# Moving an addition tree's first level into accumulating DMAs, and regrouping the score matmuls, in a two-block transformer kernel

## The chip, the cores and the metric

The kernel runs on one core of a Trainium2 chip, as one launch. The metric is device time in microseconds. TensorE (PE in the profile) multiplies matrices and writes PSUM; VectorE (DVE) and ScalarE (ACT) do elementwise work; GpSimd (POOL) and SyncE (SP) issue DMAs here and little else. Each engine takes its own instructions strictly in the order in which the program lists them, so an instruction that waits holds up everything behind it on that engine.

## The reference

With S = 2048 tokens and D = 512 channels, bf16 inputs:

```python
def _A_ref(x, wqkv, wo):              # 32 heads of 16 channels
    W, dil = 8, 2
    qkv = (x @ wqkv).reshape(B, S, 3, H, Dh) ...
    idx = pos[:, None] - (jnp.arange(W) * dil)[None, :]
    logits = einsum("bhsd,bhswd->bhsw", q, k[idx]) * Dh ** -0.5   # -1e9 where idx < 0
    o = einsum("bhsw,bhswd->bhsd", softmax(logits), v[idx])
    return o.reshape(B, S, D) @ wo
def _B_ref(x, W_gate, W_up, W_down):  # F = 1376
    gate = x @ W_gate; gate = gate * (gate > 0)
    return (gate * (x @ W_up)) @ W_down
h  = x + _A_ref(layernorm(x), wqkv, wo)
h2 = h + _B_ref(layernorm(h), W_gate, W_up, W_down)
```

Every token attends to eight earlier tokens, at distances 0, 2, ..., 14, in each of 32 small heads.

## The kernel before

The sequence is cut into four chunks of 512 tokens (`tk` 0 to 3). Channels lie on the 128 partitions in four groups `t`, so a chunk of q, k or v is 128 x 4 x 512. For each chunk the stages are:

- First layernorm: statistics by `bn_stats` on DVE (line 390), the reciprocal root by Ln and Exp on ACT (lines 400 to 407), the normalisation itself on DVE (line 425) for chunk 0 and on ACT (line 422, with the small bias made by DVE on line 411) for chunks 1 to 3, then transposes on PE (line 456) and a copy out of PSUM. `LNA` says which engine normalises: its first tuple is for this layernorm, its second for the one after attention.
- q, k and v: 48 matmuls of 128 x 512 (line 502), each group of four evicted by ACT (line 510).
- Scores: because the heads are small, q times shifted k is formed on DVE, for two channel groups and four shifts at a time (line 549, 128 x 4096 elements; four of these a chunk, two for each half `hf` of the eight shifts). PE then sums the channels of each head with a 128 x 32 selector (line 555). There are eight such matmuls for each DVE product, placed on four column strips of the array (`tile_position`), and the two products of a half accumulate in one PSUM bank.
- Softmax: Exp on ACT (line 571), the sum over shifts on PE (line 588), the reciprocal by Ln and Exp on ACT (lines 591 and 594). For chunks in `EARLY` (1 to 3) the weights are scaled by the reciprocal on DVE (line 603), for chunk 0 the result is (line 644).
- Attention output: PE spreads the weights over the channels (line 616, four row strips of the array), ACT copies them to SBUF (line 622), DVE multiplies with eight shifted copies of v for each channel group `t` (line 637, 128 x 4096) and sums the eight shifts by a tree of additions of 2048, 1024 and 512 elements (lines 640 and 663). The first addition of the tree puts the upper half of the product's buffer onto its lower half.
- Output projection (line 683) and residual. For chunks in `RPE` (chunk 0 before) the residual is added on PE with an identity matmul (line 686), and ACT copies the result to `x_sm` and sums its rows (line 692). For the others DVE adds the residual and sums the rows in one instruction out of PSUM (line 694).
- Second layernorm (its square pass on ACT, line 360), then gate and up matmuls (line 721, 88 a chunk), their evictions on ACT (lines 725 and 728), the product on DVE (line 741), the down projection (line 758), the last residual on DVE (line 769) and the store (line 773).

The order on each engine is not the order of this list. `Plan.order()` is a list scheduler: every step has an engine, an assumed duration, dependencies, buffers that it takes, and a priority out of the table `RANK` (one number for each step). Its result is written out as the program's order, so the gate, up and down matmuls of an earlier chunk stand between the attention steps of a later one, and on DVE the products `gT` of line 741 stand between attention steps. Buffers are few: nine `quad`, five `big` (the 128 x 4096 products and the spread weights), two `up_sb`, two `gr`, eight PSUM banks shared by all.

All DMAs before are issued by SP and ACT: loads at the start, all within the first 31 us, and 17 stores of the output (two of 64 KB, the rest 128 KB).

Of the kernel before, what the change touches and what calls it, by code (L numbers as in the profile page):

```python
# [8 lines left out]
P = 128  # L9
# [6 lines left out]


RANK = [
    4, 1, 5, 2, 0, 3, 47, 6, 7, 29, 171, 229, 201, 272, 727, 10, 12, 8, 11, 14,
    17, 23, 28, 32, 20, 26, 31, 16, 18, 21, 24, 27, 34, 37, 9, 13, 15, 19, 22, 25,  # L20
    30, 33, 35, 40, 45, 42, 46, 57, 38, 43, 49, 52, 56, 61, 59, 66, 70, 78, 63, 68,
    67, 74, 75, 99, 84, 157, 136, 167, 73, 180, 72, 94, 88, 101, 109, 114, 65, 83, 87, 95,
    102, 122, 165, 209, 212, 121, 131, 129, 149, 127, 134, 144, 139, 153, 151, 156, 179, 210, 222, 226,
    164, 174, 196, 206, 224, 169, 183, 200, 216, 219, 187, 202, 208, 213, 218, 237, 247, 240, 249, 230,
    238, 233, 239, 254, 267, 255, 263, 242, 258, 243, 260, 270, 273, 282, 292, 276, 283, 295, 278, 286,
    280, 287, 291, 310, 320, 319, 327, 313, 323, 316, 324, 331, 308, 333, 302, 329, 305, 332, 299, 318,
    336, 345, 361, 352, 364, 337, 360, 330, 356, 366, 328, 351, 335, 353, 342, 354, 322, 349, 359, 358,
    381, 368, 389, 363, 384, 365, 387, 393, 355, 391, 348, 382, 399, 395, 417, 709, 733, 429, 434, 716,
    736, 371, 403, 706, 732, 406, 413, 714, 735, 44, 51, 36, 50, 39, 48, 41, 53, 55, 60, 64,
    76, 81, 71, 80, 86, 82, 85, 69, 77, 89, 105, 112, 97, 107, 108, 116, 96, 104, 125, 133,  # L30
    130, 137, 128, 135, 113, 126, 143, 344, 161, 271, 140, 338, 154, 312, 124, 141, 146, 152, 192, 132,
    147, 150, 163, 195, 205, 234, 245, 264, 252, 296, 306, 301, 307, 304, 265, 284, 300, 288, 298, 350,
    362, 370, 374, 309, 321, 339, 347, 340, 367, 372, 376, 314, 326, 334, 377, 386, 397, 390, 402, 383,
    388, 380, 385, 401, 404, 405, 407, 396, 400, 392, 398, 410, 414, 420, 426, 416, 422, 430, 419, 423,
    424, 427, 432, 440, 467, 455, 476, 454, 471, 464, 480, 486, 449, 463, 437, 457, 441, 460, 448, 461,
    466, 468, 481, 439, 465, 472, 484, 451, 469, 489, 446, 473, 458, 487, 443, 477, 462, 488, 491, 475,
    501, 479, 502, 485, 507, 482, 504, 525, 492, 512, 490, 508, 528, 495, 531, 718, 737, 521, 550, 722,
    740, 516, 535, 720, 738, 547, 552, 724, 741, 62, 90, 58, 92, 54, 91, 79, 93, 98, 100, 110,
    155, 159, 145, 158, 162, 142, 148, 119, 138, 160, 198, 220, 181, 217, 176, 214, 184, 223, 166, 228,
    172, 232, 170, 231, 186, 236, 189, 444, 173, 456, 203, 379, 168, 450, 235, 244, 259, 268, 315, 227,  # L40
    256, 257, 279, 317, 325, 343, 346, 357, 409, 369, 408, 418, 411, 394, 412, 428, 436, 435, 425, 447,
    478, 494, 498, 459, 470, 493, 497, 438, 442, 445, 452, 453, 474, 483, 496, 500, 505, 511, 519, 503,
    510, 506, 515, 509, 513, 522, 523, 514, 517, 518, 520, 527, 532, 537, 541, 538, 544, 549, 542, 545,
    534, 539, 551, 585, 606, 554, 583, 572, 603, 569, 600, 612, 564, 579, 568, 581, 555, 575, 560, 576,
    584, 574, 595, 570, 594, 562, 598, 566, 591, 602, 559, 588, 578, 608, 557, 586, 601, 611, 614, 589,
    624, 605, 636, 596, 621, 593, 619, 639, 580, 641, 610, 643, 648, 625, 655, 729, 745, 615, 650, 726,
    742, 637, 654, 728, 743, 633, 657, 730, 746, 111, 118, 106, 117, 115, 123, 103, 120, 175, 177, 178,
    190, 197, 185, 193, 204, 188, 194, 182, 191, 199, 248, 262, 211, 250, 207, 241, 215, 253, 221, 275,
    274, 290, 225, 277, 246, 281, 289, 499, 251, 556, 261, 565, 269, 561, 266, 294, 293, 341, 375, 285,
    303, 297, 311, 373, 378, 415, 421, 431, 524, 433, 530, 533, 536, 526, 529, 540, 548, 546, 543, 553,  # L50
    573, 582, 590, 558, 577, 587, 597, 567, 592, 599, 607, 563, 571, 604, 609, 620, 631, 613, 618, 616,
    623, 617, 628, 634, 635, 622, 626, 627, 629, 630, 632, 638, 640, 651, 652, 645, 649, 656, 642, 646,
    644, 647, 653, 662, 676, 658, 670, 667, 679, 660, 673, 690, 674, 693, 688, 696, 668, 681, 664, 683,
    699, 669, 692, 672, 687, 685, 689, 680, 686, 697, 665, 678, 677, 684, 661, 675, 659, 671, 694, 663,
    701, 666, 703, 682, 710, 691, 705, 712, 695, 704, 698, 708, 711, 707, 717, 734, 749, 700, 719, 739,
    750, 702, 715, 731, 747, 713, 721, 744, 751, 723, 725, 748, 752,
]


# [33 lines left out]
class Plan:  # L93
# [9 lines left out]
    def add(self, key, *a, **k):  # L103
        op = Op(*a, **k)
        op.key = key
        op.seq = len(self.ops)
        if RANK:
            op.prio = RANK[op.seq]
        self.ops.append(op)
        for b in set(op.take) | set(op.use):  # L110
            b.left += 1
        return op
# [57 lines left out]
def kernel(  # L170
# [134 lines left out]


    PESUM = ()
    NWARM = 48
    DMAT = ()

    EARLY = (1, 2, 3)

    RPE, OPE = (0,), ()

    MERGE = ()

    BCN = 4

    LNA = ((0, 1, 1, 1), (0, 0, 0, 0))


    MM, TP = 0.2165, 0.07
# [14 lines left out]
    def layernorm(tk, src, dst_slots, pr, groups, on_act, residual=None):  # L337
# [7 lines left out]
        for grp in groups:  # L345
# [90 lines left out]
            if (ln, tk) in DMAT:  # L436
                for j in range(lo, hi):
                    xn, a = norm(j)

                    def f_td(j=j, xn=xn):  # L440
                        for t in range(NT):
                            nc.sync.dma_start_transpose(out=dst.t[:, t, j * P:(j + 1) * P],
                                                        in_=xn.t[:, t * P:(t + 1) * P])

                    evs.append(add((ln + "td" + gk, tk), "SP", 2.0, f_td, [a], pr, take=[dst], use=[xn], lat=2.5))
                continue
            step = 1 if tk == 0 and not residual else 2
            for j0 in range(lo, hi, step):
# [36 lines left out]
    for tk in range(NCK):  # L485
# [143 lines left out]
        for t in range(NT):  # L629
            mt = Buf(big_s)  # L630
            tpr = apr + 3 + t

            def f_mu(t=t, ab=ab, mt=mt, s0=s0):
                vb = vT[:, t, PADL + s0: PADL + s0 + CS]
                v8 = bass.AP(tensor=vb.tensor, offset=vb.offset,
                             ap=[list(vb.ap[0]), [-DIL, W]] + [list(y) for y in vb.ap[1:]])
                V.tensor_tensor(out=mt.t[:], in0=ab.t[:], in1=v8, op=ALU.mult)  # L637

            def f_a(n, mt):
                V.tensor_tensor(out=mt.t[:, 0:n, :], in0=mt.t[:, 0:n, :], in1=mt.t[:, n:2 * n, :],  # L640
                                op=ALU.add)

            def f_om(t=t, mt=mt, rc=rc, OT=OT):
                V.tensor_tensor(out=OT.t[:, t, :], in0=mt.t[:, 0, :], in1=rc.t[:], op=ALU.mult)  # L644

            m = add(("mu%d" % t, tk), "DVE", D40, f_mu, abd + [vd[t], kdone.get(("v", tk - 1, t))], tpr,
                    take=[mt], use=[ab], lat=DL)
            if (tk, t) in PESUM:
                u = Buf(od_s)

                def f_ac(mt=mt, u=u):
                    for w in range(W):
                        nc.tensor.matmul(u.t[:], lhsT=identity[:], rhs=mt.t[:, w, :],
                                         start=(w == 0), stop=(w == W - 1))

                def f_om(t=t, u=u, rc=rc, OT=OT):
                    V.tensor_tensor(out=OT.t[:, t, :], in0=u.t[:], in1=rc.t[:], op=ALU.mult)

                m = add(("ac%d" % t, tk), "PE", 8 * MM, f_ac, [m], tpr, take=[u], use=[mt], lat=PEL)
                oev[t] = add(("om%d" % t, tk), "DVE", D5, f_om, [m, rcd], tpr, take=[OT], use=[u, rc], lat=DL)  # L660
                continue
            def f_al(t=t, mt=mt, OT=OT):
                V.tensor_tensor(out=OT.t[:, t, :], in0=mt.t[:, 0, :], in1=mt.t[:, 1, :], op=ALU.add)

            for n, du in ((4, D20), (2, D10), (1, D2)):
                f = lambda n=n, mt=mt, f=f_a: f(n, mt)
                if n == 1 and tk in EARLY:
                    oev[t] = add(("tree%d" % t, tk), "DVE", du, f_al, [m], tpr, take=[OT], use=[mt], lat=DL)
                else:
                    m = add(("tree%d" % t, tk), "DVE", du, f, [m], tpr, use=[mt], lat=0.03)  # L670
            if tk not in EARLY:
                oev[t] = add(("om%d" % t, tk), "DVE", D2, f_om, [m, rcd], tpr, take=[OT], use=[mt, rc], lat=DL)
# [153 lines left out]
```

## Time and profile before

| | us |
|---|---|
| median of 8 runs | 209.39 (208.43 to 210.03) |
| time of the profiled execution | 208.91 |
| span of the profiled execution | 207.0 |
| PE busy | 199.4 (96% of the span) |
| DVE busy | 162.3 (78%) |
| ACT busy | 140.8 (68%) |
| POOL busy | 1.8 (1%) |

The span runs from the first to the last instruction; the profiled execution's time is 1.9 us above it. In the groups of instructions, a row gives the line, the engine, what is written and read, the number of instructions, their busy time, the mean duration of one, and the engine's idle time before them with its releaser. The duration of a matmul includes the pipeline's latency: matmuls of 128 x 512 that follow each other start 216 ns apart though each shows about 379 ns. A timeline row gives the start, the time to the end of the last of a merged run, and the number of instructions in it.

### The profile page before, as it was taken

What the parts mean: (1) busy time and instruction counts of PE and PEld (TensorE: products, weight loads), DVE (VectorE), ACT (ScalarE), POOL (GpSimd) and SP (SyncE); (2) the same over time, 40 slices, a digit from 0 to 9 for tenths busy, and PEclk for the clock granted to TensorE, in tenths of its full rate; (3) what the DMA queues carried; (4) which work ended last, traced back from release to release, by engine and by line L of the source; (5) the groups of instructions that cost most, each with busy time, mean ns of one, the idle gap of its engine ahead of it and who ended that gap; (6) DMA issues with size and microseconds to landing.
All of it is one profiled execution on the core that took longest, in us unless ns stands there. A gap on an engine that the chain in (4) does not pass through costs nothing.

```text
span 207.0 us, 2992 instructions
## 1 busy us (share of the span) xinstructions
PE 199.4 (96%) x1139; PEld 98.7 (48%) x1159; DVE 162.3 (78%) x241; ACT 140.8 (68%) x277; POOL 1.8 (1%) x14
## 2 busy tenths in 40 slices
PE   8699999999999999999999999999999999999994
PEld 8475344455543444444444444454444445444452
DVE  6569999999999999999879998659998564011414
ACT  3559989989999996759588558465465553535800
POOL 3000000000000000000000000000000000000000
PEclk9889999999999999999999999999999999999999
DMA  6999900000000000000010000001000100200003
GB/s 171 334 375 407 327 20 3 0 0 3 0 0 0 3 0 0 0 0 3 2 51 0 3 0 27 25 0 54 0 0 16 34 3 28 74 0 0 3 0 101
DMA packets 8813, 10.70 MB, mean 52 GB/s; under 512 B 512, under 2 KB 7648, under 8 KB 8800
## 3 DMA queue, kind: packets, MB, share of 16 engines
q1 hardware_dynamic: 7984, 9.73, 13.7%
q10 hardware_dynamic: 816, 0.79, 1.1%
q8 instruction: 9, 0.15, 0.3%
q14 instruction: 4, 0.03, 0.1%
HBM read 8.42 MB, written 2.10 MB: 51 GB/s over the span
## 4 chain that ended last, share of the span: by engine, by line
PE 64%; DVE 20%; issue 5%; DMA 5%; ACT 4%; SPq 1%; DVEq 0%
PE bank L721 37%; PE bank L758 19%; DVE big L549 7%; PE bank L683 5%; DMA x_sm<-in_A_x_dram 5%; DVE big L637 4%; DVE big L640 4%; DVE st L390 3%; ACT big L622 2%; PE bank L456 2%; ACT row L422 1%; PE bank L555 1%; ACT quad L510 1%; DVE quad L644 1%; PE bank L616 1%
## 5 line engine op out<-in xcount | busy, mean ns | idle before, releaser
L721 PE MATMUL bank<-quad,wu_sb 128*128 128x512 bf16 (+1 forms) x176 | 41.8, 379 | 0.1
L721 PE MATMUL bank<-quad,wg_sb 128*128 128x512 bf16 (+1 forms) x169 | 41.4, 379 | 0.3
L758 PE MATMUL bank<-wd_sb,gT 128*128 128x512 bf16 (+3 forms) x183 | 40.2, 366 | 0.2
L728 ACT ACTIVATE gr<-bank 128x512 bf16<-128x512 f32 (+1 forms) x44 | 25.8, 608 | 15.7 <-PE bank L721 10.9
L549 DVE TENSOR_TENSOR big<-quad,kT 128x4096 bf16<-128x4096 bf16 x16 | 35.9, 2279 | 0.1
L637 DVE TENSOR_TENSOR big<-big,vT 128x4096 bf16<-128x4096 bf16 x16 | 36.0, 2282 | 0.0
L725 ACT CAST up_sb<-bank 128x512 bf16<-128x512 f32 (+1 forms) x44 | 25.4, 589 | 14.3 <-PE bank L721 9.0
L640 DVE TENSOR_TENSOR big<-big 128x2048 bf16<-128x2048 bf16 (+2 forms) x36 | 30.6, 890 | 0.1
L741 DVE TENSOR_TENSOR gT<-gr,up_sb 128x1024 bf16<-128x1024 bf16 (+1 forms) x24 | 15.2, 642 | 18.4 <-ACT up_sb L725 11.6
L721 PEld LDWEIGHTS <-wg_sb 128*128 128x128 bf16 (+1 forms) x176 | 17.5, 100 | 20.6 <-issue 0.4
L721 PEld LDWEIGHTS <-wu_sb 128*128 128x128 bf16 (+1 forms) x176 | 17.5, 100 | 20.8 <-issue 0.8
L758 PEld LDWEIGHTS <-gT 128*128 128x128 bf16 (+1 forms) x187 | 17.8, 98 | 19.0 <-issue 0.9
L622 ACT CAST big<-bank 128x512 bf16<-128x512 f32 x32 | 16.8, 620 | 2.1 <-PE bank L616 2.1
L769 DVE TENSOR_TENSOR row<-x_sm,bank 128x512 bf16<-128x512 bf16 (+1 forms) x17 | 10.8, 653 | 9.5 <-PE bank L758 8.9
L502 PE MATMUL bank<-quad,wq_sb 128*128 128x512 bf16 (+1 forms) x70 | 17.2, 380 | 0.9 <-DMA wq_sb<-in_A_wqkv_dram 0.8
L470 ACT COPY quad<-bank 128x1024 bf16<-128x1024 bf16 (+1 forms) x16 | 15.2, 967 | 4.2 <-PE bank L456 3.9
L502 PE MATMUL bank<-quad,wk_sb 128*128 128x512 bf16 (+1 forms) x70 | 16.1, 362 | 0.1
L502 PE MATMUL bank<-quad,wv_sb 128*128 128x512 bf16 x61 | 15.9, 380 | 0.3 <-issue 0.2
L683 PE MATMUL bank<-wo_sb,quad 128*128 128x512 bf16 x62 | 15.0, 379 | 0.1
L360 ACT ACTIVATE row<-x_sm,mv 128x512 bf16<-128x512 bf16 x12 | 8.6, 718 | 8.1 <-DVE mv L352 7.8
L390 DVE BATCH_NORM_STATS2 st<-x_sm 128x6 f32<-128x512 bf16 x15 | 9.5, 679 | 4.3 <-DMA x_sm<-in_A_x_dram 4.3
L510 ACT CAST quad<-bank 128x512 bf16<-128x512 f32 x16 | 9.4, 599 | 3.8 <-PE bank L502 3.6
(72 smaller groups left out, 167.8 us busy)
## 6 DMA issues: line engine op xcount, KB each, us to landing
out_dram<-row SPq DMA_DIRECT2D x15, 128.0 KB, 1.7
x_sm<-in_A_x_dram SPq DMA_DIRECT2D x3, 512.0 KB, 10.0
wu_sb<-in_B_W_up_dram SPq DMA_DIRECT2D x1, 1376.0 KB, 10.6
wg_sb<-in_B_W_gate_dram SPq DMA_DIRECT2D x1, 1376.0 KB, 13.6
wd_sb<-in_B_W_down_dram SPq DMA_DIRECT2D x1, 1280.0 KB, 15.6
wq_sb<-in_A_wqkv_dram SPq DMA_DIRECT2D x1, 512.0 KB, 7.4
wk_sb<-in_A_wqkv_dram ACTq DMA_DIRECT2D x1, 512.0 KB, 7.8
wv_sb<-in_A_wqkv_dram SPq DMA_DIRECT2D x1, 512.0 KB, 8.6
```

The source lines that it names most:

```text
L390: V.bn_stats(out=st.t[:], in_=x_sm[:, tk * BPC + j, :])
L470: nc.scalar.copy(out=o, in_=i)
L502: nc.tensor.matmul(mm.t[:, lo:hi], lhsT=w3_sb[c][:, dt, t:D:NT], rhs=xnT.t[:, dt, lo:hi], start=(dt == 0), stop=(dt == NT - 1))
L549: V.tensor_tensor(out=pb.t[:].rearrange("p (t w) s -> p t w s", t=2), in0=q4, in1=k4, op=ALU.mult)
L622: nc.scalar.copy(out=ab.t[:, w, :], in_=bc.t[:])
L637: V.tensor_tensor(out=mt.t[:], in0=ab.t[:], in1=v8, op=ALU.mult)
L640: V.tensor_tensor(out=mt.t[:, 0:n, :], in0=mt.t[:, 0:n, :], in1=mt.t[:, n:2 * n, :], op=ALU.add)
L683: nc.tensor.matmul(od.t[:], lhsT=OT.t[:, t, j * P:(j + 1) * P], rhs=wo_sb[:, t, :], start=(t == 0), stop=(t == NT - 1 and tk not in RPE))
L721: nc.tensor.matmul(mm.t[:fs, :], lhsT=w_sb[:, dt, ft * P: ft * P + fs], rhs=hnT.t[:, dt, :], start=(dt == 0), stop=(dt == NT - 1))
L725: nc.scalar.copy(out=ub.t[:fs, i, :], in_=um.t[:fs, :])
L728: nc.scalar.activation(out=gr.t[:fs, i, :], in_=gm.t[:fs, :], func=ACT.Relu)
L758: nc.tensor.matmul(od.t[:, c0:c1], lhsT=gts[ft].t[:fs, ft % 2, j * P:(j + 1) * P], rhs=wd_sb[:fs, ft, c0:c1], start=(ft == 0), stop=(ft == ...
```

## The change

1. `DACC`: for chunks 0 to 2 and all four channel groups, the 2048-element addition of the tree is not issued on DVE. POOL issues a DMA from SBUF to SBUF that adds the upper half of the product's buffer onto its lower half (128 partitions of 4096 contiguous bytes, 524 kB). There are twelve of these. DVE's 1024-element addition of the same buffer waits for the DMA. Chunk 3 keeps all three levels on DVE.
2. `RPE` is empty: chunk 0's residual goes to DVE (line 694) like the others'.
3. `MERGE` holds all chunks: the sixteen score matmuls of a half form one step, which waits for both products of that half.
4. `LNA` is zero throughout: all normalisations are on DVE (line 425).
5. `RANK` has new numbers and 742 entries in place of 753.
6. A transposing helper (`f_td`) is rewritten; nothing uses it in either kernel, as `DMAT` is empty.

```diff
 RANK = [
-    4, 1, 5, 2, 0, 3, 47, 6, 7, 29, 171, 229, 201, 272, 727, 10, 12, 8, 11, 14,
...
+    1, 3, 4, 2, 0, 5, 56, 6, 7, 41, 155, 205, 184, 248, 716, 8, 11, 10, 12, 14,
...
 ]
...
     PESUM = ()
+
+    DACC = tuple((k, t) for k in range(3) for t in range(4))
+    DAL = 5.5
+    TDD, TDL = 2.4, 1.6
...
-    RPE, OPE = (0,), ()
-
-    MERGE = ()
+    RPE, OPE = (), ()
+
+    MERGE = (0, 1, 2, 3)
...
-    LNA = ((0, 1, 1, 1), (0, 0, 0, 0))
+    LNA = ((0, 0, 0, 0), (0, 0, 0, 0))
...
             for n, du in ((4, D20), (2, D10), (1, D2)):
                 f = lambda n=n, mt=mt, f=f_a: f(n, mt)
+                if n == 4 and (tk, t) in DACC:
+                    def f_da(mt=mt):
+                        nc.gpsimd.dma_start(mt.t[:, 0:4, :], mt.t[:, 4:8, :], accum_op=ALU.add)
+
+                    m = add(("ta%d" % t, tk), "POOL", 1.5, f_da, [m], tpr, use=[mt], lat=DAL)
+                    continue
                 if n == 1 and tk in EARLY:
```

## The prediction

> **What bounds the kernel now.** I read the busy shares and the slices first, then stretches of 10 us, the chain, and the groups of what the change touches.
>
> ```profile
> PE 199.4 (96%) x1139; PEld 98.7 (48%) x1159; DVE 162.3 (78%) x241; ACT 140.8 (68%) x277; POOL 1.8 (1%) x14
> ...
> PE   8699999999999999999999999999999999999994
> ...
> DVE  6569999999999999999879998659998564011414
> ACT  3559989989999996759588558465465553535800
> ...
> PE 64%; DVE 20%; issue 5%; DMA 5%; ACT 4%; SPq 1%; DVEq 0%
> ```
> ```profile
> 40.00:50.00 10.00, 9.95 (x59) 5.65 (x59) 10.00 (x8) 9.36 (x19) 0.00 (x0) 1.00 0.00 0
> 90.00:100.00 10.00, 9.95 (x49) 4.33 (x48) 9.06 (x18) 6.90 (x14) 0.00 (x0) 1.00 0.01 2
> 170.00:180.00 10.00, 9.95 (x58) 4.99 (x58) 3.39 (x7) 4.40 (x7) 0.00 (x0) 1.00 0.16 52
> ```
>
> The columns of the second fence are PE, PE's weight loads, DVE, ACT, POOL, the clock, the DMA share and GB/s. PE has work in every slice. DVE is as full from 20 to 90 us (10.00 of 10) and nearly idle after 165 us, while PE stays at 9.95. Busy may hide bubbles, so I also looked at starts: nearly all 128x512 matmuls start 216 ns after the one before (58.12 to 58.33 below is such a step). So PE's stream of work is the length of the kernel, and DVE counts only where PE would wait for it. PE's last matmul ends at 204.2 and 2.8 us of addition and store follow. The chain names DVE up to about 70 us because DVE's results arrive just in time there:
>
> ```profile
> 34.90 1.10 PE L555 MATMUL bank<-big,sel 128*32 128x512 bf16 x16
> 36.32 0.62 PE L555 MATMUL bank<-big,sel 128*32 128x512 bf16 x8 [0.32 <-DVE big L549]
> ...
> 57.25 1.03 PE L683 MATMUL bank<-wo_sb,quad 128*128 128x512 bf16 x4
> 58.12 0.38 PE L686 MATMUL bank<-x_sm,identity 128*128 128x512 bf16 x1
> 58.33 1.03 PE L683 MATMUL bank<-wo_sb,quad 128*128 128x512 bf16 x4
> ```
>
> The score matmuls at 36.32 waited for DVE. At 57.25 PE starts chunk 0's projection 0.27 us after DVE's last L644 (56.23 + 0.75 = 56.98): no wait, no room either.
>
> **The change part by part.** The sum is made on PE, against the profiled 208.91 us (span 207.0).
>
> *Residual of chunk 0 off PE.* Four L686 matmuls go: 4 x 0.216 = -0.86 us of PE. ACT loses four L692 (615 + 219 ns each, 3.3 us). DVE gains four L694 with their accumulator reads (687 + 83 ns, 3.1 us). Neither is full after the other edits.
>
> *Score runs.* Going from full-array matmuls into column strips, starts lie 312 ns apart and not 216, and again on leaving: 0.096 us a crossing, 0.19 a run. Example: 24.18 would be the next start after two matmuls from 23.75, the run starts at 24.28. Before there are 13 stretches of L555, after, by the program's order, 8: 5 x 0.19 = -0.96. Two places where a score run touched a spread run (one crossing shared) are lost: +0.19. Net -0.77. The price is that a merged run needs both products; DVE makes the second one 2.28 us later or more, and all queued behind on PE waits, gate and up matmuls included. The order places 3 to 6 us of q, k, v or gate matmuls between most runs, so I take its cost with the waits below.
>
> ```profile
> L549 DVE TENSOR_TENSOR big<-quad,kT 128x4096 bf16<-128x4096 bf16 x16 | 35.9, 2279 | 0.1
> L637 DVE TENSOR_TENSOR big<-big,vT 128x4096 bf16<-128x4096 bf16 x16 | 36.0, 2282 | 0.0
> L640 DVE TENSOR_TENSOR big<-big 128x2048 bf16<-128x2048 bf16 x16 | 19.0, 1217 | 0.0
> L422 ACT ACTIVATE row<-x_sm,nb,rs 128x512 bf16<-128x512 bf16 x12 | 9.5, 826 | 1.0 <-DVE nb L411 0.9
> L425 DVE TENSOR_SCALAR row<-x_sm,mv,rs 128x512 bf16<-128x512 bf16 x20 | 6.9, 407 | 4.0 <-ACT rs L407 4.0
> ```
>
> *Additions to DMA, norms to DVE.* DVE: -12 x 1.217 = -14.6 (additions), -3 x 0.15 (L411), +12 x 0.407 = +4.9 (norms), +3.1 (residuals): -7.1 us. ACT: -12 x 0.826 - 3.3 = -13.2. Neither engine sets the end, so this buys only PE's waits. By the gaps between PE's starts these are, where it waited for DVE: 0.49 us at 36.3, 0.34 and 0.25 at 69 to 72.5; and 0.24 at 22.1. Together 1.3 us. All of it may return, or merged runs may bring as much anew: +1.3 to -1.3. I take half, -0.65, since DVE is ahead of before by the following sums.
>
> *Room on DVE.* I add up what each engine has ahead of the same event, in its own order: PE at 216 ns a 128x512 matmul, DVE at the rows' means less 0.06 us of overlap. Before the last operand of chunk 0's projection, DVE had 3.4 us more than PE (and the trace shows that as just in time). After it is 42.7 of PE and 44.0 of DVE, 1.3 more: 2 us of room. For chunk 1: 3.6 more before, 1.6 after: 2 us. For chunk 2 DVE was 0.4 behind PE's sum, then 4.3: 4 us more, about 6 in all. At the start nothing is bought: chunk 1's rows land at 12.24 in either kernel.
>
> *Is the DMA hidden?* No accumulating DMA is in the trace. Each has 524 kB to read, as much to read again at the destination, and to write. The loads at the start ran at 407 GB/s, which is 1.3 us for 524 kB once: lower end, if both reads cost nothing extra. Two passes are 2.6, three 3.9, the upper end. I take D = 2.6: reading and writing overlap in a copy, and here reads double. Fixed: a 64 KB store lands 1.6 us after issue; issue is 0.33 us on SP, and I put 0.3 to 1 us for POOL, so 2.3 in all. The twelve share 16 DMA engines, so those of a chunk queue. In the new DVE order, chunk 0's four products follow each other, so DMAs are issued at 0, 2.28, 4.56 and 6.84 us. The first result is needed after three more products, a norm and a score product: 3 x 2.28 + 0.41 + 2.28 = 9.5. The fourth is needed at about 16.3; it lands at 4 x 2.6 + 2.3 = 12.7. Chunk 1: fourth needed at 15.2. Chunk 2: at 13.7, still 1.0 to spare. First results: needed at 8.6 and 8.0, landing at 4.9. All twelve are hidden at D = 2.6. POOL does nothing else and SP only stores, which share the engines but are 0.13 MB each.
>
> ```profile
> out_dram<-row SPq DMA_DIRECT2D x15, 128.0 KB, 1.7
> x_sm<-in_A_x_dram SPq DMA_DIRECT2D x3, 512.0 KB, 10.0
> ```
>
> The 10.0 us of the 512 KB loads is time in a queue behind others, not a price. The Trainium skill ("DMA: Bandwidth & Descriptors", Anatomy of one DMA) gives a POOL-issued DMA about 2.0 us plus its bytes at 436 GB/s: 3.2 us for a plain copy of this size, 4.4 with the bytes doubled, against 4.9 by the rows; both leave the sum as it is. A rule that speaks against the change: "SBUF: State Buffer", Who interferes with whom, and the box on DVE blocking DMA, say that POOL, which writes these descriptors itself, is shut out while DVE runs two-port operations such as `tensor_scalar`; for two-input `tensor_tensor` the page only infers that it is not. By the row, the 0.41 us norms are the only two-port work near. By the rule's stricter reading each issue waits out one 2.28 us product: first landing at 7.2 against 8.0 needed, hidden still. If POOL found no gap at all between products, see the third rival. No run here shows which.
>
> What stands behind a late DMA: DVE's 1024-element addition, and behind it the `gT` products of L741. These free the two `up_sb` and `gr` buffers, ACT's evictions need those, PE needs ACT's banks. So a stall past the room of 2 us is PE's loss one for one.
>
> *Sum:* -0.86 - 0.77 - 0.65 = -2.3 us: 206.6 for an execution like the profiled one. The median stood 0.48 above that one (209.39), so 207.1.
>
> **The rivals.**
>
> *Slow accumulation.* D sets it. The fourth DMA lands at 4D + 2.3 after the first issue, needed at 16.3, 15.2, 13.7. At D = 4.5 (20.3) DVE stalls 4.0, 5.1 and 6.6 us; less 2 of room once, and 6 in chunk 2: 4.0 + 5.1 - 2 + 0.6 = 7.7 us lost, less 2.3: 214.8, slower than before. It decides from D near 4: there 2.0 + 3.1 - 2 = 3.1 is lost. For it: three unoverlapped passes are 3.9, and the adder's rate is unseen. Against: the loads show the engines at 407 GB/s.
>
> *Merged runs wait.* PE's in-order wait for the second product takes 0.5 to 1 us more than the waits removed: -0.86 - 0.77 + 0.75 = -0.9, 208.5. For it: the 0.32 us wait at 36.32 is of that kind. Against: 2 us of room.
>
> *Starved POOL.* If the DMAs of a chunk can start only when DVE's row of four products ends (up to 7 us later), the fourth lands near 7 + 12.7 = 19.7: stalls 3.4, 4.5, 6.0, so 5.9 less 2.3: 213.0.
>
> *DVE's relief counts in full.* All 1.3 us of waits vanish, with some of the 0.2 us waits for ACT: -3.1, 206.3. That the change does nothing is excluded: eight score runs and no L686 stand in the program.
>
> **How the numbers follow.** My forecast (206.4 to 208.1) 0.52, relief in full 0.10, merged waits 0.12, slow accumulation 0.19, starved POOL 0.07. A change under 0.3% (0.6 us) is about what a measurement of this kernel can't tell from none. Faster: 0.52 + 0.10, half of the merged waits and a little of slow accumulation under D = 3.8, 0.69. Same: 0.10, from merged waits and D near 3.9. Slower: 0.21. The range reaches from relief in full, 205.7, to the middle of slow accumulation, 212.5 (D near 4.2); about 0.05 lies below and 0.13 above.
>
> **What would show it.** PE's count falls by 4 matmuls and the L555 group's starts fall into 8 stretches; the DVE row of 2048 elements falls from x16 to x4 and DVE's busy time by about 7 us; the DMA issues show x12 of 512 KB from POOL. Right if these land in 4 to 6 us and DVE's idle before the 1024-element additions is near nothing. Wrong if DVE waits there for DMA by several us, landings grow to 10 us or more within a chunk, or PE falls below 9.5 of 10 between 40 and 130 us.

## The result, and the profile after

The changed kernel takes 205.21 us (median of 11 runs, 203.25 to 206.04) against 209.29 us (32 runs, 208.20 to 210.14): a ratio of 0.9798, with a 95% interval of 0.9775 to 0.9821. That is faster by 4.1 us, where 2.3 were forecast, and 205.21 lies below the range that was forecast, 205.7 to 212.5. Ratios, here and below, leave out executions in a slower state of the core; medians are of all. The profiled execution took 205.21 us with a span of 203.4.

The page of the kernel after, with busy shares, slices, the chain's shares by engine, the groups that answer to those shown of before, and the DMA issues:

```profile
PE 195.3 (96%) x1134; PEld 98.4 (48%) x1155; DVE 155.1 (76%) x246; ACT 131.0 (64%) x257; POOL 12.3 (6%) x26
...
PE   8697999999999999999999999999999999999994
...
DVE  6559999999999999999659997699993662211314
ACT  4538779997389976773687379835455744566400
...
PE 78%; DVE 12%; DMA 5%; issue 2%; SPq 1%
...
L639 DVE TENSOR_TENSOR big<-big,vT 128x4096 bf16<-128x4096 bf16 x16 | 35.7, 2284 | 1.5 <-ACT big L624 1.5
L551 DVE TENSOR_TENSOR big<-quad,kT 128x4096 bf16<-128x4096 bf16 x16 | 36.1, 2282 | 0.0
...
L642 DVE TENSOR_TENSOR big<-big 128x1024 bf16<-128x1024 bf16 (+2 forms) x24 | 16.9, 728 | 0.9 <-DMA big<-big 0.7
...
big<-big POOLq DMA_DIRECT2D x12, 512.0 KB, 5.7
```

DVE works 155.1 us where it worked 162.3: 7.2 less, as summed. The twelve additions are gone (24 instructions remain in the group that had 36), and DVE waits for the DMAs that took their place 0.7 us in all (the last figure of L642's row). The chain's PE share rose from 64% to 78%, and DVE's fell from 20% to 12%. A DMA lands 5.7 us after its issue (median). Line numbers in after are larger by 2 to 8.

Where did the time go? PE's stream can be cut at the first score run, and its work in each part summed as in the forecast (0.216 us for 512 columns, a quarter of that in strips, 0.096 a crossing):

| us | before | after | difference |
|---|---|---|---|
| start to first score run | 21.01 | 22.36 | |
| PE's work in it | 11.20 | 12.28 | |
| first score run to PE's end | 183.17 | 178.16 | |
| PE's work in it | 180.20 | 177.38 | |
| all work | 191.40 | 189.66 | -1.74 |
| start beyond work | 9.81 | 10.08 | +0.27 |
| lost after the first score run | 2.8 | 0.6 | -2.2 |
| PE's end | 204.18 | 200.52 | -3.66 |

The losses leave off 0.17 us for the last matmul's latency. So of the 3.7 us between the two profiles 1.7 is PE's work, and 2.2 are losses behind the first score run that are gone, less 0.3 at the start.

The starts also tell what PE lost the 2.8 us to. Each step between two matmuls that is longer than the work is put down to the engine that released the second one:

| lost after the first score run, us | before | after | difference |
|---|---|---|---|
| to waits for DVE | 1.28 | 0.02 | -1.26 |
| to waits for ACT | 0.82 | 0.14 | -0.68 |
| in steps under 0.04 us each, without such a wait | 0.66 | 0.40 | -0.26 |

Part of the last row is the second matmul after a score run, which comes 0.03 us late in several places. The waits for ACT are short, and a timeline prints no idle time for them, because a matmul's modelled end lies past the next one's start. They show in the starts. Before:

```profile
51.49 0.59 PE L588 MATMUL bank<-ex,same 128*128 128x512 bf16 x2
52.08 1.02 PE L502 MATMUL bank<-quad,wq_sb 128*128 128x512 bf16 x4
...
65.36 0.72 PE L616 MATMUL bank<-ex,spread 32*128 32x512 bf16 x4
...
69.29 1.04 PE L456 MATMUL bank<-identity,row 128*128 128x128 bf16 x12 [0.27 <-DVE row L425]
```

After two matmuls from 51.49 the next could start at 51.92; it starts at 52.08, when ACT has copied its operand (line 470). The last of the four spread matmuls waits for ACT too (line 360), so that they take 0.72 us instead of 0.39. After, groups like these run through:

```profile
64.06 0.59 PE L590 MATMUL bank<-ex,same 128*128 128x512 bf16 x2
64.49 0.39 PE L458 MATMUL bank<-identity,row 128*128 128x128 bf16 x4
...
68.48 0.39 PE L618 MATMUL bank<-ex,spread 32*128 32x512 bf16 x4
```

### The profile page after: what moved, and what is told of

Its sections match the earlier page's. It is cut to its first block, busy times and chain, and to the rows that moved or that the text cites. A ratio compares the mean times of both kernels' runs of the same rounds, so it can differ in the third digit from the quotient of the medians.

```text
span 203.4 us, 3004 instructions
## 1 busy us (share of the span) xinstructions
PE 195.3 (96%) x1134; PEld 98.4 (48%) x1155; DVE 155.1 (76%) x246; ACT 131.0 (64%) x257; POOL 12.3 (6%) x26
## 4 chain that ended last, share of the span: by engine, by line
PE 78%; DVE 12%; DMA 5%; issue 2%; SPq 1%
PE bank L729 37%; PE bank L766 19%; PE bank L504 7%; PE bank L691 7%; DMA x_sm<-in_A_x_dram 5%; PE bank L557 4%; DVE big L639 3%; DVE big L551 3%; PE bank L458 2%; DVE big L642 2%; DVE st L394 2%; PE bank L618 1%; DVE row L429 1%; DVE quad L646 1%; PE bank L590 1%
## 5 line engine op out<-in xcount | busy, mean ns | idle before, releaser
L749 DVE TENSOR_TENSOR gT<-gr,up_sb 128x1024 bf16<-128x1024 bf16 (+1 forms) x24 | 15.3, 642 | 18.5 <-ACT gr L736 14.8
L472 ACT COPY quad<-bank 128x1024 bf16<-128x1024 bf16 (+1 forms) x16 | 15.2, 972 | 7.4 <-PE bank L458 7.3
L642 DVE TENSOR_TENSOR big<-big 128x1024 bf16<-128x1024 bf16 (+2 forms) x24 | 16.9, 728 | 0.9 <-DMA big<-big 0.7
L504 PE MATMUL bank<-quad,wq_sb 128*128 128x512 bf16 (+1 forms) x69 | 15.9, 355 | 1.6 <-DMA wq_sb<-in_A_wqkv_dram 1.5
L364 ACT ACTIVATE row<-x_sm,mv 128x512 bf16<-128x512 bf16 x16 | 11.4, 712 | 8.8 <-DVE mv L356 8.8
L671 POOL DMA_DIRECT2D big<-big x12 | 10.5, 875 | 103.9 <-DVE big L639 100.9
L691 PE MATMUL bank<-wo_sb,quad 128*128 128x512 bf16 x62 | 14.5, 379 | 0.2
```

The source lines that it names most:

```text
L472: nc.scalar.copy(out=o, in_=i)
L504: nc.tensor.matmul(mm.t[:, lo:hi], lhsT=w3_sb[c][:, dt, t:D:NT], rhs=xnT.t[:, dt, lo:hi], start=(dt == 0), stop=(dt == NT - 1))
L691: nc.tensor.matmul(od.t[:], lhsT=OT.t[:, t, j * P:(j + 1) * P], rhs=wo_sb[:, t, :], start=(t == 0), stop=(t == NT - 1 and tk not in RPE))
L749: V.tensor_tensor(out=gt.t[:fs, 0:n, :], in0=gr.t[:fs, 0:n, :], in1=ub.t[:fs, 0:n, :], op=ALU.mult)
```

## The experiments

Three theories stood after the result. **Clock:** before lost 1.6 us at the start to a half-speed PE clock (its profile shows 0.66 as the mean between 8 and 13 us, after's shows full speed), and after did not. **Waits:** PE's small waits for DVE between 20 and 75 us were more than counted, and all of them went. **Order:** it is the new instruction order, and no part alone, that pays.

### The clock at the start

```diff
-    NWARM = 48
+    NWARM = 60
+    NFILL = 14
...
+                for _ in range(NFILL if first and lo == 0 else 0):
+                    nc.tensor.matmul(mm.t[:, 0:P], lhsT=warm[:], rhs=warm[:], start=True, stop=True)
                 for dt in range(NT):
```

On the kernel before:

> The kernel before, with twelve more warm-up matmuls and fourteen idle ones (zeros, overwritten) just ahead of the first q matmul, so that PE is not idle while it waits for wq. Theory 'clock at the start' (the profile of before shows half clock from 9.0 to 12.4 us, about 1.6 us lost, the one of after does not): 1.0 to 1.7 us faster than before, 207.6 to 208.3, with full clock from about 7 us on. Theory 'waits in the middle' (the gain beyond the forecast is all from PE's waits for DVE): no change beyond 0.3 us either way.

On the kernel after:

> The same filling in the kernel after. Clock theory: the half-clock stretch is met less often by after, so it gains less here than before does, 0 to 1.0 us (204.2 to 205.2), and the difference between the two filled kernels shrinks to about 3.2 us. Waits theory: no change, and the difference stays at 4.1 us.

Measured: before filled 209.55 us (ratio to before 1.0016, 0.9986 to 1.0046), after filled 205.37 (0.9816). Both profiles have full clock, and neither kernel gained. Windows of the kernel before and of its filled version (time, PE, weight loads, DVE, ACT, POOL, clock, DMA share, GB/s), and PE's timeline of the filled one:

```profile
8.00:13.00 5.00, 4.18 (x26) 3.01 (x25) 1.26 (x4) 1.44 (x3) 0.00 (x0) 0.66 1.09 364
```
```profile
8.00:13.00 5.00, 5.00 (x53) 4.69 (x51) 1.33 (x4) 2.91 (x6) 0.00 (x0) 1.00 1.08 362
```
```profile
17.95 0.40 PE L457 MATMUL bank<-identity,row 128*128 128x128 bf16 x4 [0.33 <-ACT row L423]
18.65 0.40 PE L457 MATMUL bank<-identity,row 128*128 128x128 bf16 x4 [0.31 <-ACT row L423]
19.84 0.40 PE L457 MATMUL bank<-identity,row 128*128 128x128 bf16 x4 [0.79 <-ACT row L423]
...
21.03 0.62 PE L558 MATMUL bank<-big,sel 128*32 128x512 bf16 x8
```

With full clock PE comes earlier and then waits for chunk 1's normalised rows, until the first score run starts at 21.03, against 21.01 with the slow clock. The slow stretch lay beside another wait.

Filling adds matmuls of its own, so the other traces are the cleaner test. Those of one order have the same instructions up to the first score run, and differ in when chunk 1's rows land, between 11.53 and 13.01 us. In before's order at full clock (four of the runs below) the score run starts 8.59 us after the landing each time; in before's own profile, with the slow stretch, 8.80 (21.01 less 12.21). In after's order it is 9.77 us in four traces at full clock and 9.94 in the one with a slow stretch there. So a slow stretch costs 0.2 us in either kernel, and the clock theory falls. What moves an execution's start is the landing: in after's profile it came 0.38 us later than in before's (12.59 against 12.21).

### What DVE's relief is worth in the old order

The additions left out of the kernel before, its order kept:

```diff
-            def f_a(n, mt):
+            def f_a(n, mt, tk=tk):
+                if n == 4 and tk < 3:
+                    return
```

> The kernel before in its own order, with the twelve 2048-element additions of chunks 0 to 2 left out (the output lacks the upper four shifts there). It gives DVE back 14.6 us and changes nothing on PE. Waits theory: PE's waits for DVE between 22 and 73 us vanish, 1.3 to 2.3 us faster, 207.0 to 208.0. Forecast's term: 0.65 us faster, 208.6. Theory 'the new order did it': within 0.5 us of before, since PE's order leaves little room to use DVE's time.

Measured: 208.05 us, ratio 0.9949 (0.9925 to 0.9974), 1.3 us faster; PE's loss after the first score run fell from 2.8 to 1.9 us in the profiles: waits for DVE from 1.28 to 0.65, for ACT from 0.82 to 0.55. DVE's relief pays in the old order too, at the lower edge of the waits theory, but not the 2.2 us of after.

Chunk 0's residual moved to DVE in the kernel before, its order kept (the switch `RPX` replaces `RPE` in the code of the projection, the residual and the square pass, not in the plan):

```diff
-                           stop=(t == NT - 1 and tk not in RPE))
+                           stop=(t == NT - 1 and tk not in RPX))
-                if tk in RPE:
+                if tk in RPX:
```

> The kernel before in its own order, with only chunk 0's residual moved from PE and ACT to DVE. By the forecast's term PE loses four matmuls, -0.86 us, if DVE's 3.1 us more are covered: 208.4. If DVE is the limit around 57 to 73 us, as the chain says, the 3.1 us come through to PE for the most part: 209.5 to 211.5.

Measured: ratio 1.0177 (1.0121 to 1.0233), 3.7 us slower (2.5 to 4.9), about DVE's 3.1 us; whether it is more, six executions don't tell (median 213.88 us, 211.21 to 214.83). PE's timeline of one that took 211.89 us:

```profile
65.99 0.40 PE L617 MATMUL bank<-ex,spread 32*128 32x512 bf16 x4 [1.98 <-DVE ex L604]
...
68.13 1.02 PE L503 MATMUL bank<-quad,wv_sb 128*128 128x512 bf16 x4 [1.20 <-ACT vT L511]
...
71.18 1.04 PE L457 MATMUL bank<-identity,row 128*128 128x128 bf16 x12 [0.61 <-DVE row L426]
```

PE idles 3.8 us in three waits in a row: DVE's scaling of the weights comes late behind the residuals, then ACT's eviction, then the second layernorm's rows. Both edits together:

> The kernel before in its own order, with both edits: the twelve additions of chunks 0 to 2 left out (so the output lacks the upper four shifts there) and chunk 0's residual on DVE. The residual alone cost 4.5 us and leaving out the additions alone gained 1.3. If DVE up to 73 us is what made the residual dear, the freed 14.6 us (about 4.9 of it ahead of chunk 0's projection) cover it, and PE's 0.86 us shows: 206.8 to 207.6. If the residual is dear because of where it stands in the order (PE and ACT wait for its sums), it stays dear: 209 to 212.

Measured: 209.34 us, ratio 0.9998 (0.9966 to 1.0031). The freed time takes most of the sting (3.7 us of cost become 1.0 to 1.3 against the additions left out alone), but the residual still costs where the forecast had it save 0.86. Part of its price is its place in the order: the waits for ACT's eviction (1.14 us) and the layernorm's rows (0.61) are still there.

### The DMAs in the old order

```diff
+                if n == 4 and tk < 3:
+                    nc.gpsimd.dma_start(mt.t[:, 0:4, :], mt.t[:, 4:8, :], accum_op=ALU.add)
+                    return
```

> The kernel before in its own order, with the twelve additions issued as accumulating DMAs by POOL at the same place, nothing else moved. In this order an addition's result is used within a few us. A landing takes 4.5 to 6.7 us in after. If the order is what hides the DMAs: DVE stalls for several us a chunk, 213 to 225. If DVE's other work covers them anyway: 208 to 209.5, as with the additions left out.

Measured: 227.84 us, ratio 1.0905 (1.0842 to 1.0969). Waits in this run (engine and line, what was waited for, us in total, times, longest):

```profile
DVE big L643 <- DMA big<-big: 31.6, 9, 7.0
ACT up_sb L728 <- DVE gT L744: 16.5, 7, 6.3
```

DVE waits 31.6 us for the same DMAs for which it waits 0.7 in after. ACT's evictions wait behind it for the `gT` products, as the forecast named. The order is what hides them. Not all of the 18.5 us that this kernel is slower is waiting: after the long waits PE's clock is granted at half for 6.8 us twice (from 59.8 and from 141.7 us), which by the doubled steps between matmuls is worth about 4.5 us (an estimate).

### The parts taken back out of the kernel after

All four keep after's order. First, additions back on DVE at the place where the DMAs were issued:

```diff
-                        nc.gpsimd.dma_start(mt.t[:, 0:4, :], mt.t[:, 4:8, :], accum_op=ALU.add)
+                        V.tensor_tensor(out=mt.t[:, 0:4, :], in0=mt.t[:, 0:4, :], in1=mt.t[:, 4:8, :], op=ALU.add)
```

> The kernel after in its own order, with the twelve additions back on DVE, in the place where the DMAs were issued; no accumulating DMA. DVE gets 14.6 us back, 4.9 a chunk. If the room is 2 us in chunks 0 and 1 and about 6 in chunk 2, PE loses 2.9 and 4.9 us and nothing or little in chunk 2: 211 to 214. If the additions hardly matter on their own (the gain is that of the order and of PE's edits): within 1 us of after, 205 to 206.

Measured: 217.42 us, ratio to before 1.0368 (1.0327 to 1.0409), 12.2 above after. DVE's 14.6 us came through to PE almost whole, in chunk 2 as well (2.75 us of wait at 130.1 us, for ACT behind `gT`), where I had expected nothing. At chunk 0's projection the room was what had been summed:

```profile
57.21 3.19 PE L691 MATMUL bank<-wo_sb,quad 128*128 128x512 bf16 x14 [2.53 <-DVE quad L646]
```

4.9 us more on DVE, 2.53 us of wait here, beside 1.30 us at 46 us for a normalised row that stands behind an addition.

Second, the residual back on PE and ACT:

> The kernel after in its own order, with chunk 0's residual back on PE (four matmuls) and ACT, off DVE. PE is the bound in after: +0.86 us, 206.1. If DVE's 3.1 us were still paid for by PE: no change or faster, 203 to 205.2.

Measured: 206.56 us (ratio to before 0.9881, 0.9823 to 0.9939), 1.35 above after, with 0.86 expected. The profile has PE's end at 201.90 against 200.52. Of that, 0.59 came before the first score run, from rows that landed 0.42 us later and a slow stretch of the clock (0.17), neither of which the residual makes; from there to PE's end it is 178.95 us against 178.16, 0.79 more, the four matmuls' work.

Third, each merged score run broken in the middle:

```diff
+                def f_brk(p=prd, sc=sc):
+                    p[0][2]()
+                    nc.tensor.matmul(sc.t[:, 0:16], lhsT=warm[:], rhs=p[0][1].t[:, 0, 0:16],
+                                     start=False, stop=False)
+                    p[1][2]()
```

> The kernel after with each of its eight merged score runs broken once in the middle by one small full-array matmul that adds zeros. By the price of a crossing (0.096 us, two for a break) and 0.03 to 0.06 us for the small matmul: 8 x 0.22 to 0.25 = +1.8 to +2.0 us, 207.0 to 207.2. If waits cover the crossings: under +0.5 us.

Measured: 207.36 us (0.9886, 0.9847 to 0.9924), 2.15 above after, 0.27 us a break. Behind the first score run, free of the start's scatter, the profiles have 179.92 us against 178.16: 0.22 a break, as expected for two crossings and the small matmul. A crossing costs what the starts show, with nothing beside it to cover it.

Fourth, normalisations of chunks 1 to 3 back on ACT:

```diff
+                if tk and not residual:
+                    if not made:
+                        made.append(1)
+                        f_nb()
+                    nc.scalar.activation(out=xn.t[:], in_=x, func=ACT.Identity,
+                                         bias=nb.t[:, j:j + 1], scale=rs.t[:, j:j + 1])
```

> The kernel after in its own order, with the first layernorm's normalisation of chunks 1 to 3 back on ACT (twelve of 0.83 us, and the three small biases on DVE). DVE gains 4.4 us. If DVE's room of 2 us is what matters, no loss: within 0.5 us of after. If ACT's place for them is the price (PE waited 1.9 us at 17 to 20 us for ACT's rows in the filled kernel before, 1.7 us for DVE's rows in after): +0.5 to +2.5 us, from PE's transposes of chunk 1.

Measured: 211.87 us (1.0136, 1.0072 to 1.0201), 6.7 above after, far more than either expectation. In the profile the score run starts 11.72 us after chunk 1's rows land, 2.0 later than in after; the rest comes behind it. The run's waits:

```profile
PEld L467 <- ACT row L432: 4.4, 5, 1.8
DVE big L648 <- ACT big L633: 4.3, 3, 2.7
```

In after's order twelve activations of 0.83 us stand on ACT between the copies of the spread weights (L633), so both PE's transposes and DVE's products wait for ACT. That ACT had room by its total (64% busy) says nothing about that stretch.

### How late a DMA may come

```diff
+                        nc.gpsimd.tensor_copy(out=cf[:, 0:1], in_=mt.t[:, 7, 0:1])
+                        for _ in range(15):
+                            nc.gpsimd.iota(ci[:], pattern=[[0, 1]], base=0, channel_multiplier=1)
                         nc.gpsimd.dma_start(mt.t[:, 0:4, :], mt.t[:, 4:8, :], accum_op=ALU.add)
```

> The kernel after with each accumulating DMA held back on POOL by a one-column copy of its product and fifteen small index fills (about 2.1 us, each waiting for the one before; the fourth of a chunk some 3 to 4 us late, as POOL falls behind DVE's 2.28 us pace). In after DVE waited 0.7 us in all for these DMAs. If there is the room of 1 to 3 us that the forecast worked out: DVE waits 1 to 3 us a chunk and PE loses under 2 us, 205 to 207. If after stands just at the edge: PE loses 2 us in each of chunks 0 and 1, 208 to 210.

Measured: 237.94 us (1.1342, 1.1271 to 1.1413). The dose was larger than meant. POOL's timeline of this run:

```profile
35.25 2.18 POOL L671 CAST cf<-big 128x1 f32<-128x1 bf16 x1 [32.80 <-DVE big L639]
37.38 2.89 POOL L673 IOTA ci<- 128x1 int32 x15
40.39 1.01 POOL L674 DMA_DIRECT2D big<-big  x1
...
52.91 0.87 POOL L674 DMA_DIRECT2D big<-big  x1
```

The first DMA is issued at 40.39 and not 36.25, the fourth at 52.91 and not 42.80, 10 us late. DVE waits 30.2 us for them over three chunks, and the kernel is 32.7 us slower. So this run doesn't measure where the room ends. It shows that past it most of DVE's stall is passed on, in chunk 2 too. PE's waits behind the first score run come to about 26 us, and about 7 more (an estimate from the doubled steps between matmuls) to the clock: four times, amid such waits, it is granted at half, the first time from 55.5 us:

```profile
54.96 0.39 PE L694 MATMUL bank<-wo_sb,quad 128*128 128x512 bf16 x1 [2.47 <-DVE quad L646]
59.13 3.17 PE L694 MATMUL bank<-wo_sb,quad 128*128 128x512 bf16 x7 [3.79 <-DVE quad L646]
```
```profile
56.00:62.00 6.00, 2.87 (x7) 1.04 (x8) 5.54 (x8) 1.07 (x2) 0.00 (x0) 0.50 0.16 31
```

After's own profile says how near the edge it stands. Between a DMA's landing and the start of the addition that needs it lie at least 0.55 us in chunk 0 and 0.84 in chunk 1. In chunk 2 the last DMA lands late, and DVE waits for it:

```profile
122.72 0.69 DVE L642 TENSOR_TENSOR big<-big 128x1024 bf16<-128x1024 bf16 x1 [0.70 <-DMA big<-big]
```

No wait of PE for DVE follows from these 0.7 us.

### An earlier start

After's profile has long waits of PE left only ahead of the first score run. One of them is for chunk 1's rows:

```profile
17.50 0.81 PE L504 MATMUL bank<-quad,wv_sb 128*128 128x512 bf16 x3
19.44 0.40 PE L458 MATMUL bank<-identity,row 128*128 128x128 bf16 x4 [1.13 <-DVE row L429]
20.08 0.40 PE L458 MATMUL bank<-identity,row 128*128 128x128 bf16 x4 [0.25 <-DVE row L429]
```

The rows stand on DVE behind a 2.28 us score product. Chunk 1's load is moved ahead of that of the v weights, and the rows ahead of the product:

```diff
         for c, q in enumerate((nc.sync, nc.scalar, nc.sync)):
+            if c == 2:
+                nc.sync.dma_start(x_sm[:, BPC:2 * BPC, :], x_rows[:, BPC:2 * BPC, :])
...
-        for tk in range(1, NCK):
+        for tk in range(2, NCK):
...
     todo = plan.order()
+    at = next(i for i, op in enumerate(todo) if op.key == ("pr1", 0))
+    early = [op for op in todo[at:] if op.key == ("xxn", 1)]
+    todo = todo[:at] + early + [op for op in todo[at:] if op not in early]
```

> The kernel after with chunk 1's rows loaded ahead of the v weights and the last three of its four normalisations placed ahead of DVE's first score product. In after PE waits 1.7 us at 18 to 20 us for those rows, behind that product. If the wait is only moved to the score runs, which need the product: 0 to 0.5 us faster. If it goes: 1.0 to 1.7 us faster, 203.5 to 204.2, faster than both kernels.

Measured: 203.84 us (203.67 to 204.22), ratio to before 0.9746 (0.9706 to 0.9785). DVE's timeline now has the four rows ahead of all products, and PE reaches the score run at 20.90 and not 22.36 (21.58 to 22.40 in the four traces of after's order at full clock):

```profile
10.52 1.88 DVE L396 BATCH_NORM_STATS2 st<-x_sm 128x6 f32<-128x512 bf16 x3 [2.29 <-DMA x_sm<-in_A_x_dram]
...
14.73 1.36 DVE L431 TENSOR_SCALAR row<-x_sm,mv,rs 128x512 bf16<-128x512 bf16 x4
16.01 8.89 DVE L553 TENSOR_TENSOR big<-quad,kT 128x4096 bf16<-128x4096 bf16 x4
```

The executions of after spread from 203.25 to 206.04 us, and two of its eleven lie under this median, so the 1.4 us between the medians rest on few executions; the earlier score run is plain in the traces. The two moves were not tried apart.

## Why the prediction was right or wrong

**PE as the bound, DVE's totals: right.** DVE fell by 7.2 us, with 7.1 forecast. Residual and crossings were forecast at -1.63 us of PE work and are -1.74 by the program; with the residual put back PE took 0.79 us longer behind the first score run, and 0.22 a break with the score runs broken.

**The DMA term: right.** I took D = 2.6 us for the accumulation. Held apart by POOL's delay, the packets of one DMA span 2.8 us (41.96 to 44.73, worked out from the packets' records), and it lands 4.5 to 4.6 us after issue (5.0 once), where 4.9 was forecast. The fourth of chunk 0 landed at 49.23, 12.98 us after the first issue at 36.25; 12.7 was forecast. So slow accumulation and starved POOL did not happen. The margin was thinner than forecast, since the results were needed earlier: the fourth of each chunk at 14.7, 13.8 and 13.4 us after the first issue (16.3, 15.2 and 13.7 forecast), the last of these after the wait of 0.7. POOL's issue took 0.86 to 1.01 us, at the bracket's upper end, while DVE ran products back to back.

**The term that failed: "Together 1.3 us. ... I take half, -0.65".** It is the size of PE's waits, and two steps of it went wrong. The first is the halving. PE's waits for DVE in before are 1.28 us by the trace, as summed, and 0.02 in after: all of them went, and merged runs brought none anew. The sums of DVE's room, right there in the text, said that DVE comes 2 us earlier than before at both projections, which leaves nothing of waits this small. The second is that "this buys only PE's waits" was counted for DVE alone: ACT, relieved of 13.2 us in the same paragraph, was put at nothing, and PE's waits for ACT fell by 0.68. With 0.26 in small steps that makes -2.2, not -0.65. That the sum of 1.3 is right is in part luck: the 0.24 at 22.1 was no wait, but a matmul that the trace doesn't show (four weight loads, three matmuls), while waits of 0.09 each at the transposes of 69.6 and 69.9 us were left out. "DVE's relief counts in full" was the nearer rival; it was too small because it allowed under 0.2 us for ACT. (The range's lower end calls 205.7 relief in full, where that rival's own sum gives 206.3.)

With -2.2 in place of -0.65 the sum is -3.8, or -3.9 with the crossings as counted by the program. The profiles have -3.66 chiefly because in after's chunk 1's rows landed 0.38 us later; with equal landings it would be -4.0, and the medians have -4.1 (-3.75 to -4.7 by the interval).

**"At the start nothing is bought": right**, and better than I knew: before's slow clock, in which a later reader may see 1.6 us to be had, is covered by chunk 1's rows up to 0.2 us.

**Room in chunk 2: wrong, without harm.** I gave it 6 us, from total sums that count idle time as room. Additions put back cost nearly all of their 14.6 us and delays of the DMAs reached PE there too, so chunk 2 has little more room than the others.

**What was missing:** that the parts lean on each other. The sum took each edit's price alone. In the old order the residual on DVE costs 3.7 us and the DMAs cost 18.5; in the new order taking out either the DMAs or DVE's normalisations costs 12.2 and 6.7. The terms held because the new order gives each its place, which I had read off for the DMAs but for no other part. What the order is worth by itself, and merged score runs without it, no run shows.

## What to carry to other kernels

Measure an engine's losses as its span minus the sum of its work, and put each down to its releaser, whichever engine that is: listed waits leave out the short ones, and a sum for the one engine that the change is about leaves out the others. Before costing a move between engines, read the stretch of the in-order queue where it lands: by its total of busy time ACT had room for twelve activations, and their price was 6.7 us; the residual, forecast to save 0.86 us, cost 3.7 in the old order. A transfer that replaces an instruction is only as good as the work that the order puts between issue and use: here 6.2 to 8.5 us of it hid 4.5 to 6.7 us of DMA but for one wait of 0.7, and without it the same twelve DMAs cost 18.5 us.

## What the hardware showed

An accumulating DMA from SBUF to SBUF of 524 kB kept the DMA engines 2.8 us, or 190 GB/s of result, under half the 407 GB/s of the loads. Queued at 1.9 to 2.4 us intervals, landing grows from 4.65 to 6.43 us over four of them. The starvation rule weighed in the forecast can now be split by the trace. In the delayed run POOL's one-column copy took 2.2 us at the head of chunks 0 and 2 and 7.18 at that of chunk 1:

```profile
84.47 7.18 POOL L671 CAST cf<-big 128x1 f32<-128x1 bf16 x1 [30.69 <-DVE big L639]
```

DVE ran two-input products without a gap from 82.12 to 92.21 us, and the copy ended at 91.65. The nine other copies took 0.51 to 1.04 us. Issuing a DMA took 0.86 to 1.01 us beside the same products, and 0.87 where DVE was idle (94.84 in that run). So POOL's read of SBUF was held up, and its writing of descriptors was not. The Trainium skill ("SBUF — State Buffer", Who interferes with whom) states the first for instructions with two inputs in SBUF, and infers the second for `tensor_tensor`.
